# Fewer small VectorE instructions in a routing search, and one instead of two per first-layer block, in a mixture-of-experts kernel

## The chip, the cores and the metric

The kernel runs on one core of a Trainium2 chip, as one launch. The metric is the device time of the launch in microseconds (us). Before the change three runs took 705.04, 704.34 and 704.64 us; their median is 704.64 us.

## The reference

A linear attention (retention) over 8 batches, 8 heads, 576 positions and a head width of 64 gives 4,608 tokens of 512 numbers. These go through a mixture of 8 experts. Routing is global and greedy: all pairs of a token and an expert are taken in the order of falling gate value; a token goes to the expert of its first pair that finds the expert not yet full (576 tokens each). Cut to what matters:

```python
logits = x @ w_gate                       # 4608 x 8
order = np.argsort(-logits.flatten())
for idx in order:
    tok, e = (int(idx) // E, int(idx) % E)
    if assigned[tok] >= 0 or counts[e] >= cap:
        continue
    assigned[tok] = e
    counts[e] += 1
for e in range(E):
    mask = assigned == e
    h = np.maximum(x[mask] @ w1[e], 0.0)  # 512 -> 1024
    out[mask] = h @ w2[e]                 # 1024 -> 512
```

## The kernel before, in words

**Stages.** The attention runs first, to about 200 us of the profile. Its results go to a buffer in memory (xd), and the gate values stay on the chip as 36 columns of 128 tokens. Then experts are taken one after another, in the order in which they fill up. Everything from about 229 us on is the expert stage.

**An expert.** Its 576 tokens are fetched by an indirect transfer (`gather`, line 934), transposed on TensorE in five steps (`transposes`, line 945) and split there into a high and a low part: ScalarE writes the high part xh (line 958), VectorE the rest xl (line 959). The five steps take their PSUM banks in turn under the names t, h0, h1, t, h0; t exists once, so the fourth transpose waits until line 959 has emptied the bank of the first. Weights are split the same way (`conv`, line 914: two ScalarE instructions and an adding transfer issued by GpSimd). A product in full precision is then three products of parts.

The first layer (`l1`, line 963) has 16 blocks: f from 0 to 7 (128 hidden units each), s = 0 for tokens 0 to 255 and s = 1 for tokens 256 to 575. A block is 12 products on TensorE (line 984) into a bank h0 or h1, of which there are two each. ScalarE then writes the Relu's high part into hb (line 988), and VectorE the low part, the Relu less the high part (line 991): one instruction for s = 0, two for s = 1, of 256 and of 64 tokens. The low part of the last 64 tokens lies right behind their high part (columns 576 to 639), so that the second layer can take both as one operand of 128 columns.

The second layer (`l2`, line 1006) goes over five tiles of tokens, t = 0 to 4, the last with 64 tokens; each has eight groups f of three products, or two in the last tile (line 1023). ScalarE or ScalarE and VectorE (lines 1040, 1042, 1043) take the result out, and GpSimd sends it to its rows in memory.

**A round of routing.** Round p finds the expert that fills up next and its list of tokens, while TensorE works on expert p - 1. It has three parts. The search (`search`, line 285; round 0 has its own, `search_first`) finds the value at which the expert fills up, digit by digit, in seven levels of 32 or 16 candidates. In a level, VectorE makes a table G of which token reaches which candidate (`reach`, line 161); TensorE counts per expert with nine products of four columns each (line 312), which leaves four partial counts in four blocks of 32 partitions of one PSUM bank (`own`); VectorE adds them up with the (negative) room of each expert (lines 315 to 319), takes the largest over the experts (325), compares it with zero into a column copied to all four blocks of partitions (327), transposes the column (328) and adds it up to the digit j (329). The next level's values v follow (297, 307). The digits are cut out of the values once a round (lines 154, 155), most of them in level 0 behind its table, and copied to bf16 as D (304). After the last level `f` is written by four comparisons (332). Then `members` and `listing` (lines 354, 388) mark and number the tokens and write the list with counts on TensorE (381, 417), and `leave` (448) takes the expert out and looks up each token's best remaining expert (lines 455 to 206).

**What sets the order.** The program is written out in one order, and each engine works through its own part of it in that order. Where the routing's steps stand among the products of the experts is set by a planner, `Mixer` (line 845). It keeps a time for TensorE (t) and one for VectorE (v). Every three products of the first layer add 320 or 400 to t, every group of the second 650 (`adv`); every piece of VectorE work adds its cost to v (`vec`). The routing is a generator that yields, ahead of each count on TensorE, the cost of the VectorE work before it, in ns; the planner multiplies it by 1.0 for rounds 0 and 1 and by 1.2 from round 2 on, and lets the count out as soon as its t has passed the resulting due time:

```python
            d, s.pe = next(s.side)
            s.vec(d * s.slack)
            s.ready = s.v + 150
```

A level after the first is given 2050 + 19 K for K candidates (line 309). The planner also sets when the tokens are fetched, once the list is there, and when the transposes start (line 1035).

Of the kernel before, what the change touches and what calls it, by code (L numbers as in the profile page):

```python
# [10 lines left out]
F32 = mybir.dt.float32  # L11
F32R = mybir.dt.float32r
BF16 = mybir.dt.bfloat16
I32 = mybir.dt.int32
ALU = mybir.AluOpType
AF = mybir.ActivationFunctionType
AX = mybir.AxisListType
# [46 lines left out]
def widths(shifts):  # L64
    return [1 << (a - b) for a, b in zip([32] + shifts[:-1], shifts)]
# [16 lines left out]
class Route:  # L82
# [202 lines left out]
    def search(s):  # L285
        nc, V, pool, ps = s.nc, s.nc.vector, s.pool, s.ps
        SH, KK = LATER, widths(LATER)
        for _ in s.ordered():
            pass
        s.dig(0)  # L290
        for it, K in enumerate(KK):
            last = it == len(SH) - 1
            v2 = pool.tile([128, 36, 2], BF16, name="v", bufs=2)
            v = v2[:, :, 0]
            if it:

                V.tensor_scalar(v2, u[:, :, None].to_broadcast([128, 36, 2]), j, None, op0=ALU.subtract)
            else:
                V.tensor_copy(v2, s.dg[:, 0, :, None].to_broadcast([128, 36, 2]))
            s.reach(0, 36, K, v2, ALU.is_le)  # L300
            if it == 0:
                for k in range(1, 7):
                    s.dig(k)
                V.tensor_copy(s.D[:, 1:], s.dg[:, 1:])
            if not last:
                u = pool.tile([128, 36], F32, name="u")
                V.scalar_tensor_tensor(u, v, float(KK[it+1]), s.D[:, it+1], op0=ALU.mult, op1=ALU.add)

            yield (2050 + 19*K if it else 1350), 310
            cp = ps.tile([128, 32], F32, name="r")  # L310
            for c in range(0, 36, 4):
                nc.tensor.matmul(cp, s.G[:, c:c+4].rearrange("p c k -> p (c k)"), s.oh[:, c:c+4, :], start=(c == 0), stop=(c == 32))
            own = [cp[32*c:32*c+32, 8*c:8*c+8] for c in range(4)]
            cs, ct = pool.tile([32, 8], F32, name="cs"), pool.tile([32, 8], F32, name="ct4")
            V.tensor_tensor(cs, own[0], s.nr[:32], op=ALU.add)
            V.tensor_copy(ct, own[1])
            V.tensor_tensor(cs, own[2], cs, op=ALU.add)
            V.tensor_tensor(ct, own[3], ct, op=ALU.add)
            V.tensor_tensor(cs, cs, ct, op=ALU.add)
            if last:  # L320
                break

            mc, mq = pool.tile([32, 1], F32, name="mc"), pool.tile([128, 1], F32, name="mq")
            tc, j = pool.tile([128, 32], F32, name="tc"), pool.tile([128, 1], F32, name="j")
            V.tensor_reduce(mc, cs, axis=AX.X, op=ALU.max)
            for q in range(0, 128, 32):
                V.tensor_scalar(mq[q:q+32], mc, 0.0, float(KK[it+1]), op0=ALU.is_ge, op1=ALU.mult)  # L327
            V.transpose(tc, mq.to_broadcast([128, 32]))
            V.tensor_reduce(j, tc[:, 1:K], axis=AX.X, op=ALU.add)

        for q in range(0, 128, 32):
            V.tensor_scalar(s.f[q:q+32, :8], cs, 0.0, None, op0=ALU.is_ge)
        tf, cf = pool.tile([128, 32], F32, name="tc"), pool.tile([128, 32], F32, name="cf")
        nk, nf = pool.tile([128, 1], F32, name="nk"), pool.tile([128, 1], F32, name="nf")
        w = pool.tile([128, 8], F32, name="w8")
        s.ge = pool.tile([128, 2, 36], F32, name="ge")
        s.gt, s.eq = s.ge[:, 0], s.ge[:, 1]
        V.transpose(tf, s.f)
        V.tensor_reduce(nk, tf[:, :K], axis=AX.X, op=ALU.add)
        V.transpose(cf, nk.to_broadcast([128, 32]))  # L340
        V.tensor_reduce(nf, cf[:, :8], axis=AX.X, op=ALU.max)
        V.scalar_tensor_tensor(w, cf[:, :8], nf, s.dec, op0=ALU.is_equal, op1=ALU.mult)
        V.tensor_scalar(s.gt, v, nf, -1.0, op0=ALU.subtract, op1=ALU.is_gt)
        V.tensor_scalar(s.eq, v, nf, -1.0, op0=ALU.subtract, op1=ALU.is_equal)
        s.pick(w)
# [530 lines left out]
def moe(tc, nc, P, R, xd, w1_d, w2_d, out, mix):  # L876
    V, A, T = nc.vector, nc.scalar, nc.tensor
# [84 lines left out]

    def l1(e, tr):

        hb = P['w'].tile([128, 8, 1152], F32R, name="hb", bufs=1)
        order = [(f, s) for f in range(8) for s in range(2)]
        if e == 0:
            order[1:3] = order[2], order[1]
        for i, (f, s) in enumerate(order):
            wh, wl = [w.rearrange("p (f d m) -> p f d m", f=2, d=4)[:, f % 2] for w in W1[e, f // 2]]  # L970
            if i == 0 and e:
                next(tr, None)
                next(tr, None)
            elif i == 1:
                for _ in tr:
                    pass
            xh, xl = XH[e], XL[e]
            c, n = ((slice(0, 256), 256), (slice(256, 576), 320))[s]
            ps = P['ps'].tile([128, n], F32, name="ph", tag=f"h{s}", bufs=2)
            terms = [(w[:, d], x[:, d, c]) for d in range(4) for w, x in ((wh, xh), (wh, xl), (wl, xh))]  # L980
            if e == 0 and f < 2:
                terms = terms[0::3] + terms[2::3] + terms[1::3]
            for k, (w, x) in enumerate(terms):
                T.matmul(ps, w, x, start=(k == 0), stop=(k == 11))  # L984
                if k % 3 == 2:
                    mix.adv(320 + 80*s)
                    gather(e + 1)
            A.activation(hb[:, f, c], ps, AF.Relu)  # L988
            for a, b in ((0, 256),) if s == 0 else ((0, 256), (256, 320)):
                to = (640 if a == 0 else 64) + 256*s  # L990
                V.scalar_tensor_tensor(hb[:, f, to+a:to+b], ps[:, a:b], 0.0, hb[:, f, 256*s+a:256*s+b].bitcast(F32),  # L991
                                       op0=ALU.max, op1=ALU.subtract)
            mix.vec(340 + 140*s)
            if s and f in (1, 2, 4, 6) or e == 0 and i < 3:
                conv()
        return hb
# [9 lines left out]
    def l2(e, hb):  # L1006
        tr = iter(())
        late = []
        want = 4*(e + 1 < E)
        wait = 0  # L1010
        for t in range(5):
            n = 128 if t < 4 else 64
            ps = P['ps'].tile([128, DM], F32, name="py", tag="y", bufs=2)
            c = slice(128*t, 128*t+n)
            k, last = 0, 23 if t < 4 else 15
            for f in range(8):
                wh, wl = [w[:, (f % 2)*512:(f % 2)*512+512] for w in W2[e, f // 2]]

                h = hb[:, f]
                for a, w in ((h[:, c], wh), (h[:, 640+128*t:768+128*t], wh), (h[:, c], wl)) if t < 4 else \  # L1020
                        ((h[:, 512:640], wh), (h[:, c], wl)):
                    m = a.shape[1]
                    T.matmul(ps[:m], a, w, start=(k == 0), stop=(k == last), skip_group_check=True)  # L1023
                    k += 1
                mix.adv(650)
                gather(e + 1)
                wait -= 1

                soon = state['listing'] == e + 1 and not ready(e + 1)
                if want and wait <= 0 and e + 1 in regs and not soon:  # L1030
                    conv()
                    want, wait = want - 1, 6
                if late and not soon:
                    late.pop(0)()
                if e + 1 in XG and e + 1 not in XH and mix.t > state['arrives']:
                    tr = transposes(e + 1)
                next(tr, None)
            y = P['w'].tile([128, DM], F32, name="yt", bufs=3)
            if t < 4:
                A.activation(y, ps, AF.Copy)  # L1040
            else:
                A.activation(y[:n], ps[n:], AF.Copy)  # L1042
                V.tensor_tensor(y[:n], y[:n], ps[:n], op=ALU.add)  # L1043
            late.append(lambda t=t, y=y, n=n: scatter(e, t, y, n))
        for f in late:
            f()
        for _ in range(want):
            conv()
        if e + 1 < E and e + 1 not in XH:
            mix.drain(lambda: ready(e + 1))  # L1050
            gather(e + 1)
            tr = transposes(e + 1)
        return tr
# [84 lines left out]
```

## Time and profile before

| | us |
|---|---|
| median of three runs | 704.64 |
| profiled execution | 710.73 |
| its span, first to last instruction | 709.0 |
| TensorE products busy | 662.8 |
| VectorE busy | 434.9 |
| ScalarE busy | 315.4 |
| GpSimd busy | 182.7 |

The profile is one execution. Rows of its timeline give the start and the time of an instruction, its engine (PE is TensorE, DVE is VectorE, ACT is ScalarE, POOL is GpSimd), its line in the kernel, what it writes and from what, and in brackets how long the engine had stood idle before it and what ended that. Instructions of one kind in a row are merged (x4). Rows of groups give the count, the busy time and the mean of one in ns, and the idle time before them. A row of waits gives who waited for whom, the sum in us, the number of times and the longest. The granted clock is the share of TensorE's full clock that it was allowed.

### The profile page before, as it was taken

How to read it: one execution, taken by the hardware profiler on the slowest of the kernel's cores; microseconds unless marked ns; L12 is line 12 of the kernel's file. 1: busy time of each engine (PE TensorE's matmuls, PEld its weight loads, DVE VectorE, ACT ScalarE, POOL GpSimd, SP SyncE). 2: the span in 40 equal slices, each digit the busy share in tenths (PEclk: the TensorE clock that was granted, in tenths of full speed). 3: DMA queues.
4: the chain of work that ended last, by engine and by line, in shares of the span. 5: the costliest groups of instructions: out<-in, count | busy, mean ns of one | idle time of the engine just before them, and what ended most of it. 6: DMA issues, size and time to landing. Idle time of an engine off the chain costs nothing.

```text
span 709.0 us, 14398 instructions
## 1 busy us (share of the span) xinstructions
PE 662.8 (93%) x5435; PEld 578.1 (82%) x5435; DVE 434.9 (61%) x1660; ACT 315.4 (44%) x551; POOL 182.7 (26%) x236
## 2 busy tenths in 40 slices
PE   5999999999986899999999998899999999999995
PEld 5998988988764887897788778788978988988984
DVE  4456766867845698888588788769977321221200
ACT  2555555554412733555244515533551571571521
POOL 3121212122203202515213314124133233332111
PEclk9999999999966999999899999999999999999999
DMA  7986688784416754978928946884794886886421
GB/s 227 337 308 230 218 273 302 242 286 145 135 48 213 177 122 161 237 192 237 250 53 229 233 120 156 208 194 132 156 246 143 202 213 188 204 200 198 90 60 37
DMA packets 53429, 134.74 MB, mean 190 GB/s; under 512 B 6128, under 2 KB 22512, under 8 KB 53360
## 3 DMA queue, kind: packets, MB, share of 16 engines
q1 hardware_dynamic: 38400, 81.91, 34.1%
q0 software_dynamic: 14960, 51.91, 33.1%
q8 instruction: 43, 0.70, 0.4%
q14 instruction: 26, 0.21, 0.1%
HBM read 81.90 MB, written 18.87 MB: 142 GB/s over the span
## 4 chain that ended last, share of the span: by engine, by line
PE 59%; DVE 18%; issue 9%; DMA 8%; ACT 2%; SPq 2%; POOL 1%; POOLq 0%; DVEq 0%; ACTq 0%
PE py L1023 19%; PE ph L984 14%; PE pA L573 7%; PE pX L624 4%; DMA raw<-in_w 3%; PE pS L589 3%; PE pX L614 3%; DVE hb L991 2%; DMA w1l<-raw 2%; DVE G L161 2%; PE pT L653 1%; PE pT L690 1%; PE pt L956 1%; DVE mq L327 1%; PE r L270 1%
## 5 line engine op out<-in xcount | busy, mean ns | idle before, releaser
L1023 PE MATMUL py<-w2h,hb 128*128 128x512 f32 x576 | 191.1, 404 | 0.0
L984 PE MATMUL ph<-xh,w1h 128*128 128x320 f32 (+1 forms) x512 | 153.1, 303 | 4.7 <-DVE hb L991 2.5
L984 PE MATMUL ph<-xh,w1l 128*128 128x320 f32 (+1 forms) x512 | 149.5, 296 | 0.0
L984 PE MATMUL ph<-xl,w1h 128*128 128x320 f32 (+1 forms) x512 | 149.4, 296 | 0.0
L1023 PE MATMUL py<-w2l,hb 128*128 128x512 f32 (+1 forms) x320 | 126.5, 395 | 0.2 <-DMA w2l<-raw 0.2
L1023 PEld LDWEIGHTS py<-w2h,hb 128*128 128x128 f32 x576 | 105.5, 191 | 21.3
L984 PEld LDWEIGHTS ph<-xh,w1h 128*128 128x128 f32 x512 | 96.8, 190 | 6.9 <-ACT w2l L928 2.7
L988 ACT ACTIVATE hb<-ph 128x256 fp32r<-128x256 f32 (+1 forms) x128 | 51.8, 408 | 111.8 <-PE ph L984 105.2
L984 PEld LDWEIGHTS ph<-xl,w1h 128*128 128x128 f32 x512 | 96.4, 190 | 0.3
L984 PEld LDWEIGHTS ph<-xh,w1l 128*128 128x128 f32 x512 | 96.3, 189 | 0.1
L991 DVE SCALAR_TENSOR_TENSOR hb<-ph,hb 128x256 fp32r<-128x256 f32 (+1 forms) x192 | 58.5, 352 | 56.5 <-ACT hb L988 54.4
L573 PE MATMUL pA<-qin,kz 128*128 128x128 f32 x576 | 75.8, 288 | 6.7 <-DMA qin<-in_qk 5.3
L595 ACT ACTIVATE S<-pS,cst 64x128 f32<-64x128 f32 x128 | 46.4, 362 | 75.5 <-PE pS L589 73.9
L573 PEld LDWEIGHTS pA<-qin,kz 128*128 128x128 f32 x576 | 70.5, 200 | 9.2 <-ACT kz L514 7.1
L1000 POOL DMA_INDIRECT out_y<-yt,idx x40 | 40.3, 1008 | 117.2 <-ACT yt L1040 78.3
L1023 PEld LDWEIGHTS py<-w2l,hb 128*128 128x128 f32 (+1 forms) x320 | 57.6, 180 | 14.0 <-DMA w2l<-raw 0.7
L1040 ACT ACTIVATE yt<-py 128x512 f32<-128x512 f32 x32 | 19.1, 598 | 107.3 <-PE py L1023 84.4
L555 POOL TENSOR_TENSOR ks<-nin,cst 128x512 f32<-128x512 f32 (+1 forms) x33 | 33.2, 1025 | 129.5 <-DMA nin<-in_vk 85.1
L577 DVE TENSOR_TENSOR am<-pA,cst 128x512 f32<-128x512 f32 (+1 forms) x80 | 48.4, 633 | 23.9 <-PE pA L573 23.5
L929 POOL DMA_DIRECT2D w2l<-raw x32 | 28.8, 900 | 126.5 <-ACT hb L988 116.3
L940 POOL DMA_INDIRECT xg<-xd,idx x40 | 41.0, 1025 | 67.2 <-issue 30.0
L1043 DVE TENSOR_TENSOR yt<-yt,py 64x512 f32<-64x512 f32 x8 | 5.4, 678 | 69.5 <-ACT yt L1042 69.4
(179 smaller groups left out, 977.0 us busy)
## 6 DMA issues: line engine op xcount, KB each, us to landing
raw<-in_w SPq DMA_DIRECT2D x64, 512.0 KB, 5.6
w2l<-raw POOLq DMA_DIRECT2D x32, 512.0 KB
w1l<-raw POOLq DMA_DIRECT2D x31, 512.0 KB
kin<-in_qk SPq DMA_DIRECT2D x14, 576.0 KB
qin<-in_qk SPq DMA_DIRECT2D x14, 576.0 KB
vin<-in_vk SPq DMA_DIRECT2D x14, 576.0 KB, 5.3
nin<-in_vk SPq DMA_DIRECT2D x14, 512.0 KB, 5.0
xd<-xr SPq DMA_DIRECT2D x36, 192.0 KB, 3.1
```

Source lines behind the costliest of these rows:

```text
L555: nc.gpsimd.tensor_tensor(KS[u][:, a:b], LD[u, 'n'].rearrange("p (a d) -> p a d", d=64)[:, a:b], ks[:, u % HP, a:b, None].to_broadcast([12 ...
L573: nc.tensor.matmul(pa[:, j, h], KZ[u % 2][:, h, s], LD[u, 'q'][:, s], start=True, stop=True)
L577: nc.vector.tensor_tensor(am[:, :n], pa[:, :n], m[:, None, 2*hp:2*hp+2, :].to_broadcast([128, n, 2, 128]), op=ALU.mult)
L595: nc.scalar.activation(st[64*h:64*h+64, :, 64*h:64*h+64], PS[u][64*h:64*h+64], AF.Copy, scale=ss[64*h:64*h+64, hp, c:c+1])
L624: nc.tensor.matmul(px[64*h:64*h+64, :], v[:, blk*128+64*h:blk*128+64*h+64], AM[g][:, h, :], start=False, stop=blk < 8, skip_group_check=True)
L929: nc.gpsimd.dma_start(lo, raw, accum_op=ALU.add)
L940: nc.gpsimd.indirect_dma_start(out=xg[:n, j, :], out_offset=None, in_=xd[:, :], in_offset=bass.IndirectOffsetOnAxis(ap=found[e][:n, j:j+1] ...
L984: T.matmul(ps, w, x, start=(k == 0), stop=(k == 11))
L988: A.activation(hb[:, f, c], ps, AF.Relu)
L991: V.scalar_tensor_tensor(hb[:, f, to+a:to+b], ps[:, a:b], 0.0, hb[:, f, 256*s+a:256*s+b].bitcast(F32), op0=ALU.max, op1=ALU.subtract)
L1000: st = nc.gpsimd.indirect_dma_start(out=out[:, :], out_offset=bass.IndirectOffsetOnAxis(ap=found[e][:n, t:t+1], axis=0), in_=y[:n], in_off ...
L1023: T.matmul(ps[:m], a, w, start=(k == 0), stop=(k == last), skip_group_check=True)
```

## The change

In a search level three of the four partial counts are taken off the room (`cs` is then what the others leave), and the fourth is compared with that, once for each block of 32 partitions; the largest of the flags over the experts replaces the largest of the counts and the comparison with zero. The factor between levels goes from the flags to the values: D holds digits divided by K, u is a plain sum, and v is (u - j) times K. After the last level the same four comparisons stand for the ones at line 332. The planner's cost of a level falls from 2050 + 19 K to 1700 + 19 K. In the first layer, the low part of 320 tokens is one instruction; the low parts now lie together at columns 576 to 1151, and ScalarE writes the high part of the last 64 tokens a second time behind them, at columns 1152 to 1215. The second layer's operand for the last tile takes these.

```diff
@@ search
-                V.tensor_scalar(v2, u[:, :, None].to_broadcast([128, 36, 2]), j, None, op0=ALU.subtract)
+                V.tensor_scalar(v2, u[:, :, None].to_broadcast([128, 36, 2]), j, float(K), op0=ALU.subtract, op1=ALU.mult)
...
-                V.tensor_copy(s.D[:, 1:], s.dg[:, 1:])
+                for a, b in ((1, 4), (4, 7)):
+                    V.tensor_scalar(s.D[:, a:b], s.dg[:, a:b], 1.0/KK[a], None, op0=ALU.mult)
...
-                V.scalar_tensor_tensor(u, v, float(KK[it+1]), s.D[:, it+1], op0=ALU.mult, op1=ALU.add)
-
-            yield (2050 + 19*K if it else 1350), 310
+                V.tensor_tensor(u, v, s.D[:, it+1], op=ALU.add)
+
+            yield (1700 + 19*K if it else 1350), 310
...
-            cs, ct = pool.tile([32, 8], F32, name="cs"), pool.tile([32, 8], F32, name="ct4")
-            V.tensor_tensor(cs, own[0], s.nr[:32], op=ALU.add)
-            V.tensor_copy(ct, own[1])
-            V.tensor_tensor(cs, own[2], cs, op=ALU.add)
-            V.tensor_tensor(ct, own[3], ct, op=ALU.add)
-            V.tensor_tensor(cs, cs, ct, op=ALU.add)
+            cs = pool.tile([32, 8], F32, name="cs")
+            V.scalar_tensor_tensor(cs, s.nr[:32], -1.0, own[0], op0=ALU.mult, op1=ALU.subtract)
+            for x in own[1:3]:
+                V.tensor_tensor(cs, cs, x, op=ALU.subtract)
+            for q in range(0, 128, 32):
+                V.tensor_tensor(s.f[q:q+32, :8], own[3], cs, op=ALU.is_ge)
...
-            V.tensor_reduce(mc, cs, axis=AX.X, op=ALU.max)
-            for q in range(0, 128, 32):
-                V.tensor_scalar(mq[q:q+32], mc, 0.0, float(KK[it+1]), op0=ALU.is_ge, op1=ALU.mult)
+            V.tensor_reduce(mq, s.f[:, :8], axis=AX.X, op=ALU.max)
             V.transpose(tc, mq.to_broadcast([128, 32]))
             V.tensor_reduce(j, tc[:, 1:K], axis=AX.X, op=ALU.add)
...
-        for q in range(0, 128, 32):
-            V.tensor_scalar(s.f[q:q+32, :8], cs, 0.0, None, op0=ALU.is_ge)
@@ l1
-        hb = P['w'].tile([128, 8, 1152], F32R, name="hb", bufs=1)
+        hb = P['w'].tile([128, 8, 1216], F32R, name="hb", bufs=1)
...
-            for a, b in ((0, 256),) if s == 0 else ((0, 256), (256, 320)):
-                to = (640 if a == 0 else 64) + 256*s
-                V.scalar_tensor_tensor(hb[:, f, to+a:to+b], ps[:, a:b], 0.0, hb[:, f, 256*s+a:256*s+b].bitcast(F32),
-                                       op0=ALU.max, op1=ALU.subtract)
+            V.scalar_tensor_tensor(hb[:, f, 576+256*s:576+256*s+n], ps, 0.0, hb[:, f, c].bitcast(F32), op0=ALU.max, op1=ALU.subtract)
+            if s:
+                A.activation(hb[:, f, 1152:1216], ps[:, 256:320], AF.Relu)
             mix.vec(340 + 140*s)
@@ l2
-                for a, w in ((h[:, c], wh), (h[:, 640+128*t:768+128*t], wh), (h[:, c], wl)) if t < 4 else \
-                        ((h[:, 512:640], wh), (h[:, c], wl)):
+                for a, w in ((h[:, c], wh), (h[:, 576+128*t:704+128*t], wh), (h[:, c], wl)) if t < 4 else \
+                        ((h[:, 1088:1216], wh), (h[:, c], wl)):
```

More of the change, by code (lines that the diff above doesn't have):

```diff
@@ L313, in search @@
             own = [cp[32*c:32*c+32, 8*c:8*c+8] for c in range(4)]
-            cs, ct = pool.tile([32, 8], F32, name="cs"), pool.tile([32, 8], F32, name="ct4")
-            V.tensor_tensor(cs, own[0], s.nr[:32], op=ALU.add)
-            V.tensor_copy(ct, own[1])
-            V.tensor_tensor(cs, own[2], cs, op=ALU.add)
-            V.tensor_tensor(ct, own[3], ct, op=ALU.add)
-            V.tensor_tensor(cs, cs, ct, op=ALU.add)
+            cs = pool.tile([32, 8], F32, name="cs")
[4 more added lines that the diff above has]
+                V.tensor_tensor(s.f[q:q+32, :8], own[3], cs, op=ALU.is_ge)
             if last:
                 break
-            mc, mq = pool.tile([32, 1], F32, name="mc"), pool.tile([128, 1], F32, name="mq")
+            mq = pool.tile([128, 1], F32, name="mq")
             tc, j = pool.tile([128, 32], F32, name="tc"), pool.tile([128, 1], F32, name="j")
-            V.tensor_reduce(mc, cs, axis=AX.X, op=ALU.max)
-            for q in range(0, 128, 32):
-                V.tensor_scalar(mq[q:q+32], mc, 0.0, float(KK[it+1]), op0=ALU.is_ge, op1=ALU.mult)
+            V.tensor_reduce(mq, s.f[:, :8], axis=AX.X, op=ALU.max)
             V.transpose(tc, mq.to_broadcast([128, 32]))
             V.tensor_reduce(j, tc[:, 1:K], axis=AX.X, op=ALU.add)
-        for q in range(0, 128, 32):
-            V.tensor_scalar(s.f[q:q+32, :8], cs, 0.0, None, op0=ALU.is_ge)
         tf, cf = pool.tile([128, 32], F32, name="tc"), pool.tile([128, 32], F32, name="cf")
```

## The prediction

> **What bounds the kernel now.** I read the page first, then who waited for whom, with TensorE as the one that waits and from 229 us on, where the experts run:
>
> ```profile
> PE r L312 <- DVE G L161: 6.2, 9, 1.7
> PE pt L956 <- DVE xl L959: 4.5, 4, 2.0
> PE ph L984 <- DVE hb L991: 2.5, 3, 1.1
> PE ph L984 <- ACT hb L988: 1.2, 1, 1.2
> PE r L381 <- DVE sc L374: 0.9, 1, 0.9
> PE ph L984 <- ACT xh L958: 0.9, 1, 0.9
> PE r L417 <- DVE rh L413: 0.5, 1, 0.5
> ...
> ```
>
> Columns: microseconds in all, times, the longest. TensorE is hardly ever short of work in this stage: with two small ones left out, all its waits come to 17.2 us, and almost all of them are for VectorE. The change leaves every product of the expert layers as it was, so it can pay only through these waits and what they trail. Next, TensorE's and VectorE's timelines at the two longest waits for xl:
>
> ```profile
> 331.29 0.62 PE L1023 MATMUL py<-w2h,hb 128*128 128x512 f32 x2
> ...
> 331.97 0.39 PE L312 MATMUL r<-oh,G 128*128 128x32 bf16 x9
> ...
> 337.74 0.75 PE L956 MATMUL pt<-ident,xg 128*128 128x128 f32 x4 [2.00 <-DVE xl L959]
> ...
> 455.57 0.53 PE L956 MATMUL pt<-ident,xg 128*128 128x128 f32 x4 [1.88 <-DVE xl L959]
> ```
> ```profile
> 333.54 0.16 DVE L315 TENSOR_TENSOR cs<-r,room 32x8 f32<-32x8 f32 x1 [0.74 <-PE pt L956]
> ...
> 336.99 1.29 DVE L959 TENSOR_TENSOR xl<-pt,xh 128x512 fp32r<-128x512 f32 x2
> ```
>
> A level's count (331.97) goes out right ahead of the first transpose of the next expert's tokens. VectorE works through the whole level, from 333.54 to 336.99, before it comes to the first xl; the fourth transpose needs the bank which that xl empties, and waits. Then the clock falls. Windows at these two places and at a third, the granted clock third from the right, behind the busy times:
>
> ```profile
> 334.34:337.75 3.41, 1.41 (x10) 0.83 (x8) 3.13 (x13) 3.21 (x5) 2.08 (x5) 1.00 1.07 205
> 453.80:457.21 3.41, 1.64 (x11) 1.21 (x11) 3.29 (x7) 0.60 (x1) 0.00 (x0) 1.00 1.01 187
> 245.59:249.00 3.41, 1.69 (x18) 1.43 (x17) 3.02 (x16) 0.38 (x1) 0.38 (x1) 1.00 1.03 269
> 249.00:252.41 3.41, 3.41 (x34) 3.41 (x31) 3.03 (x17) 2.60 (x4) 0.00 (x0) 1.00 0.93 247
> 337.75:344.60 6.85, 6.85 (x29) 4.94 (x30) 3.03 (x9) 2.87 (x4) 1.95 (x3) 0.50 1.03 234
> 457.20:460.60 3.40, 3.40 (x10) 2.71 (x9) 0.68 (x2) 2.28 (x3) 0.70 (x2) 0.50 0.71 258
> ```
>
> After 3.41 us with only 1.41 and 1.64 of TensorE work the granted clock was 0.50, for 6.85 and 3.40 us; after a stretch with 1.69 it stayed at 1.00. Half of 6.85 and of 3.40, 5.1 us, went there. The expert stage's whole bill is thus 17.2 + 5.1 = 22.3 us.
>
> [...]
>
> **What a level costs and saves.** VectorE's rows of a level with 32 candidates, then groups by form:
>
> ```profile
> 245.14 0.42 DVE L991 SCALAR_TENSOR_TENSOR hb<-ph,hb 128x256 fp32r<-128x256 f32 x1 [2.14 <-ACT hb L988]
> 245.48 0.14 DVE L315 TENSOR_TENSOR cs<-r,room 32x8 f32<-32x8 f32 x1
> ...
> 247.26 0.21 DVE L328 STREAM_TRANSPOSE tc<-mq 128x32 f32<-128x32 f32 x1
> ```
> ```profile
> L991 DVE SCALAR_TENSOR_TENSOR hb<-ph,hb 128x256 fp32r<-128x256 f32 x128 | 52.0, 421 | 56.5 <-ACT hb L988 54.4 <-ACT w2l L928 1.6
> ...
> L991 DVE SCALAR_TENSOR_TENSOR hb<-ph,hb 128x64 fp32r<-128x64 f32 x64 | 13.7, 214 | 0.0
> ...
> L318 DVE TENSOR_TENSOR ct<-r,ct 32x8 f32<-32x8 f32 x42 | 7.0, 168 | 1.3
> ...
> L319 DVE TENSOR_TENSOR cs<-cs,ct 32x8 f32<-32x8 f32 x42 | 6.5, 154 | 1.4
> ```
>
> The ten instructions from L315 up to the transpose take 1.78 us, 0.18 each. Afterwards there are eight: three sums, four comparisons, one maximum. At 0.18 that is 1.44; the comparisons read PSUM, as L318 does (168 ns; L319, from SBUF, 154), which adds 0.06: 1.50. Saved 0.28, or 0.38 if the four, which do not wait for one another, follow at bare duration. I take 0.33, 14 us over 42 levels. The product in L307 becomes a sum and v's line gets a second scalar; no instruction is added there, so I cost both at nothing. D takes two instructions for one, 0.2 once a round by L318 and L319, behind the first count.
>
> [...]
>
> In the first layer a block of 320 tokens takes one L991 of 421 + 64/192 of (421 - 214) = 490 ns instead of 635: 0.14 saved, 9 us over 64 blocks. ScalarE gets 64 copies of 64 columns. No row shows one; the nearest are L991's forms, so between 0.21 and 0.42, and I take 0.25, near the smaller. They stand behind a Relu, where ScalarE mostly waits for TensorE. Only where a weight conversion follows (four blocks an expert) does the next Relu, and the L991 queued on it, come that much later: 0.5 us in all. Without that cover they would be 16.
>
> **Where the levels land.** VectorE's saving of some 22 us does not reach the end by itself. What counts is TensorE's order, which the planner sets, and it takes 350 ns off a level (420 from round 2 on, with its factor of 1.2), about what a level really gains. Adding up its costs with 1700 for 2050 gives the new places: round 1 ends four product groups earlier, and the lead grows to 5.8, 8.0, 9.8, 14.3 and 19.3 planner microseconds by the ends of rounds 2 to 6. Each search meets other work than before. TensorE's pace, the rows to compare with, and VectorE's tail of a listing:
>
> ```profile
> 238.92 0.31 PE L984 MATMUL ph<-xh,w1h 128*128 128x320 f32 x1
> ...
> 240.67 0.28 PE L984 MATMUL ph<-xh,w1h 128*128 128x256 f32 x1
> ...
> 242.11 0.31 PE L984 MATMUL ph<-xh,w1h 128*128 128x320 f32 x1
> ...
> 242.56 0.39 PE L312 MATMUL r<-oh,G 128*128 128x32 bf16 x9
> ...
> 248.83 0.39 PE L312 MATMUL r<-oh,G 128*128 128x32 bf16 x9 [1.72 <-DVE G L161]
> ...
> 256.98 0.39 PE L312 MATMUL r<-oh,G 128*128 128x32 bf16 x9 [0.26 <-DVE G L161]
> ...
> 260.88 0.39 PE L312 MATMUL r<-oh,G 128*128 128x32 bf16 x9 [0.22 <-DVE G L161]
> ...
> 483.51 0.85 PE L417 MATMUL r<-rh,G 128*128 128x160 bf16 x9 [0.49 <-DVE rh L413]
> ...
> 492.96 0.39 PE L312 MATMUL r<-oh,G 128*128 128x32 bf16 x9
> ...
> 498.06 0.39 PE L312 MATMUL r<-oh,G 128*128 128x32 bf16 x9 [0.54 <-DVE G L161]
> ...
> 512.82 0.47 PE L956 MATMUL pt<-ident,xg 128*128 128x128 f32 x4
> ...
> 516.57 0.54 PE L956 MATMUL pt<-ident,xg 128*128 128x128 f32 x4 [0.40 <-DVE xl L959]
> ```
> ```profile
> 489.56 0.46 DVE L206 TENSOR_TENSOR oh<-t,mx 128x288 bf16<-128x288 bf16 x1
> ...
> 490.05 1.22 DVE L991 SCALAR_TENSOR_TENSOR hb<-ph,hb 128x256 fp32r<-128x256 f32 x4
> ```
>
> First-layer blocks last 1.75 and 1.44 (238.92 to 242.11), a second-layer group 0.68 (331.29 to 331.97) or two thirds of it in the last tile; first to fourth transpose takes 3.35 unhindered (512.82 to 516.57, less 0.40).
>
> *Levels, 6.2 now.* Round 1: level 2 moves up by six products. VectorE is held until 245.14 + 0.34 by ScalarE as before, so its count comes 0.33 earlier, at 248.5; TensorE asks three quarters of a 1.75 block, one of 1.44 and a quarter of 1.75 after the last count (242.56 + 0.24), at 246.0: 2.5. The next four stand 3.0 to 3.4 apart, and VectorE needs 3.90 (256.98 to 260.88) less 0.33 and 0.14: 0.3 each. Round 1: 3.7. Level 0 to level 1 took 5.10 in the first layer (492.96 to 498.06), which becomes 4.85, and 4.3 without L991s; in round 4 the step now runs from the third product of block 11 to the sixth of block 13, in round 5 from the end of block 3 to the third of block 6, in round 6 over one whole group and four of the last tile. With the count's own 0.24 that gives TensorE 3.9, 3.8 and 2.8: 0.95, 1.05 and 1.5 of wait. Level 0 follows its listing by 9.45 (483.51 to 492.96), 8.2 without the 1.22 of L991s; round 5's now has TensorE time of 8.0 in the first layer, round 6's 7.6 in the second, round 2's 7.0 as before: 1.5, 0.6, 1.2. Other levels, by the same sums: 2.0. Together 12.5.
>
> *Transposes, 4.8 now with a small one for cs.* In experts 1 and 3 no level stands right ahead of the first transpose any more: the 2.00 and 1.88 go. But round 6's listing now stands six products before expert 4's second layer. VectorE's tail of a listing ends 6.5 us after the listing starts (483.51 to 490.02); with one L991 and one xl the bank is free at 7.6, and the fourth transpose asks at 0.7 + 0.9 + 0.7 + 3.35 = 5.6: 2.0, where 0.40 stood. Small ones elsewhere 1.1. Together 3.1.
>
> *First-layer banks, 3.7 now.* A listing or members step in the first layer holds back L991 and so a bank. Round 4's two leave the first layer; round 3 comes to the same blocks: 1.9. *Members and listings, 1.4:* both leave the spots that waited; 0.2. *Start, 1.1* as before. *ScalarE's copies* 0.5.
>
> *Clock, 5.1 now.* The waits of 2.5 and 2.0 leave 0.9 to 1.4 us of work in a window that holds them whole, more in one that splits them; two falls of 3.4 us with a chance of two thirds each: 2.3.
>
> Sum: 12.5 + 3.1 + 1.9 + 0.2 + 1.1 + 0.5 + 2.3 = 21.6 against 22.3, so 0.7 us less. This is made within the profiled execution of 710.73 us; the median of the runs is 704.64, no row tells where the 6 us between them lie, and I carry the difference over as it is: 703.9.
>
> **The rivals.** *The new level waits are half as long.* VectorE's queue ahead of a level may be shorter than in the rows I compared with. Rounds 5 and 6 then pay about half of their 5.5, and no window falls low enough for the clock: 21.6 - 2.8 - 2.3 = 16.5, 698.8 us. For it: VectorE is lighter throughout. Against: its order is fixed, and what it waits for (ScalarE at 245.14) stays.
>
> *The clock falls at the new waits as it did at 337.75.* Where expert 4's wait and round 1's leave under 1.65 us of work in their windows and the fall lasts 6.85, it costs 6.8 instead of 2.3: 26.1, 708.4, slower. For it: 2.5 and 2.0 are as long as 2.00 and 1.88. Against: 1.72 did not trip it.
>
> [...]
>
> **How the numbers follow.** A measurement of this kernel tells 0.2%, 1.4 us, from no change. My forecast, 703.9, has 0.47, on a range of its own from 701 to 706.5: 0.20 faster, 0.22 same, 0.05 slower. The halved waits have 0.27, all faster; the clock 0.18 and the comparisons 0.08, all slower. That makes 0.47 faster, 0.22 same, 0.31 slower. The range holds the first two rivals' times with about a microsecond to spare: 698 to 709.5.
>
> **What would show it.** From the first sum to the transpose 1.4 to 1.5 us instead of 1.78; L991 in a form of 320 near 490 ns; no wait near 2 us for xl in experts 1 and 3, one in expert 4; a wait near 2.5 in round 1; waits for G of about 12 us. I am wrong if those waits are not there, if the 320-wide L991 or ScalarE's copies hold banks, or if the clock falls at more than two places.

## The result and the profile after

The changed kernel takes 758.64 us (median of four runs, 756.66 to 761.76) where the kernel before took 704.49 beside it: a ratio of 1.076, 95% interval 1.072 to 1.080. It is slower by 54 us. The forecast was 703.9 with a range up to 709.5, so it failed by size and by sign. Two executions of the experiments below, one of 723.75 us with the copy first and one of 919.1 us with one column, lay more than 1.5% above the fastest of their kernel and are in no ratio.

The profiled execution took 756.66 us. Its span and mean granted clock, first after, then before, from the view of cores:

```profile
core 0: 754.9 us, clock 0.947
```
```profile
core 0: 709.0 us, clock 0.974
```

The expert stage's waits of TensorE, after the change, from 229 us on:

```profile
PE r L313 <- DVE G L161: 20.4, 16, 3.1
PE pt L954 <- DVE xl L957: 14.6, 5, 5.1
PE ph L982 <- ACT hb L989: 7.2, 3, 3.2
PE pt L954 <- DMA xg<-xd,idx: 1.5, 1, 1.5
PE ph L982 <- ACT xh L956: 0.6, 1, 0.6
PE py L1020 <- DMA w2l<-raw: 0.5, 2, 0.3
PE ph L982 <- DVE hb L987: 0.4, 2, 0.2
```

They come to 45.2 us, against 17.2 before: 28.0 more. The lower clock accounts for the rest, as an estimate from the two means: 0.053 of 754.9 is 40.0 us of lost clock, 0.026 of 709.0 is 18.4, so 21.6 more. Together that is 49.6, for a span that grew by 45.9. TensorE has the same work and is kept from it longer.

Who keeps it is shown by the second and third row of the list of all waits of the kernel after:

```profile
POOL w2l L927 <- ACT hb L986: 157.1, 31, 10.2
ACT hb L989 <- DVE hb L987: 108.2, 64, 6.5
DVE hb L987 <- ACT hb L986: 97.2, 59, 3.4
```

L989 is ScalarE's new copy of 64 columns. It waits for VectorE in each of its 64 blocks, 108.2 us in all. Before, ScalarE waited for VectorE nowhere in the first layer but once, for 2.2 us. In the trace each of the 64 copies waits for the semaphore that L987 raises; this has nothing to do with what the copy needs, which is a bank that TensorE has filled.

What one such wait does, around 387 us. ScalarE's, VectorE's and TensorE's timelines of the kernel after:

```profile
380.25 0.70 ACT L986 ACTIVATE hb<-ph 128x256 fp32r<-128x256 f32 x2
387.47 0.22 ACT L989 ACTIVATE hb<-ph 128x64 fp32r<-128x64 f32 x1 [6.53 <-DVE hb L987]
387.59 1.05 ACT L922 ACTIVATE w2h<-raw 128x1024 fp32r<-128x1024 f32 x1
388.54 1.05 ACT L926 ACTIVATE w2l<-raw 128x1024 fp32r<-128x1024 f32 x1
389.49 0.71 ACT L986 ACTIVATE hb<-ph 128x256 fp32r<-128x256 f32 x2
```
```profile
380.99 0.15 DVE L443 TENSOR_TENSOR room<-room,r 128x8 f32<-128x8 f32 x1
...
386.45 0.46 DVE L206 TENSOR_TENSOR oh<-t,mx 128x288 bf16<-128x288 bf16 x1
386.94 0.49 DVE L987 SCALAR_TENSOR_TENSOR hb<-ph,hb 128x320 fp32r<-128x320 f32 x1
389.90 0.82 DVE L987 SCALAR_TENSOR_TENSOR hb<-ph,hb 128x256 fp32r<-128x256 f32 x2 [2.46 <-ACT hb L986]
```
```profile
387.75 0.41 PE L982 MATMUL ph<-xh,w1h 128*128 128x320 f32 x1 [3.19 <-ACT hb L989]
```

It is a circle. VectorE is in the tail of a listing (380.99 to 386.91), and its L987 stands behind that. The copy waits for L987 for 6.53 us, and the two conversions and the next block's Relu stand behind the copy. VectorE, done at last, has to wait for that Relu: 2.46 us. TensorE's next block waits for the bank that the copy holds (3.19 us). Before the change ScalarE did not stop for a busy VectorE. VectorE was in the tail of a listing from 484.43 to 490.02 there, and ScalarE wrote the Relus of the next blocks as soon as TensorE had them:

```profile
487.34 0.44 ACT L988 ACTIVATE hb<-ph 128x320 fp32r<-128x320 f32 x1 [1.38 <-PE ph L984]
488.78 0.38 ACT L988 ACTIVATE hb<-ph 128x256 fp32r<-128x256 f32 x1 [1.00 <-PE ph L984]
```

The search itself did what was said of it. The first block shows a level of the kernel after on VectorE, the second two groups of its first layer:

```profile
240.96 0.14 DVE L317 SCALAR_TENSOR_TENSOR cs<-room,r 32x8 f32<-32x8 f32 x1
241.13 0.34 DVE L319 TENSOR_TENSOR cs<-cs,r 32x8 f32<-32x8 f32 x2
241.51 0.72 DVE L321 TENSOR_TENSOR f<-r,cs 32x8 f32<-32x8 f32 x4
242.26 0.16 DVE L327 TENSOR_REDUCE mq<-f 128x1 f32<-128x8 f32 x1
242.46 0.21 DVE L328 STREAM_TRANSPOSE tc<-mq 128x32 f32<-128x32 f32 x1
```
```profile
L987 DVE SCALAR_TENSOR_TENSOR hb<-ph,hb 128x320 fp32r<-128x320 f32 x64 | 31.1, 486 | 20.0 <-ACT hb L986 19.7
...
L989 ACT ACTIVATE hb<-ph 128x64 fp32r<-128x64 f32 x64 | 14.4, 224 | 108.2 <-DVE hb L987 108.2
```

From the start of the first sum to the start of the transpose it takes 1.50 us, where it was 1.78. The instruction for 320 tokens takes 486 ns and the copy 224.

### The profile page after: what moved, and what is told of

The parts are those of the page before. It is cut to its first block, busy times and chain, and to the rows that moved or that the text cites. A ratio compares the mean times of both kernels' runs of the same rounds, so it can differ in the third digit from the quotient of the medians.

```text
span 754.9 us, 14265 instructions
## 1 busy us (share of the span) xinstructions
PE 679.2 (90%) x5431; PEld 592.5 (78%) x5435; DVE 421.2 (56%) x1518; ACT 324.7 (43%) x615; POOL 182.7 (24%) x236
## 4 chain that ended last, share of the span: by engine, by line
PE 53%; DVE 23%; ACT 9%; issue 6%; DMA 5%; POOL 2%; SPq 1%; POOLq 0%; DVEq 0%; ACTq 0%
PE py L1020 20%; PE ph L982 10%; PE pA L571 6%; DVE hb L987 4%; PE pX L622 3%; PE pS L587 3%; DVE G L161 2%; DVE f L321 2%; PE pX L612 2%; ACT w2h L922 2%; ACT w2l L926 2%; DMA nin<-in_vk 2%; PE pt L954 1%; PE pT L651 1%; ACT hb L986 1%
## 5 line engine op out<-in xcount | busy, mean ns | idle before, releaser
L1020 PE MATMUL py<-w2h,hb 128*128 128x512 f32 x576 | 195.7, 413 | 0.0
L982 PE MATMUL ph<-xh,w1h 128*128 128x320 f32 (+1 forms) x512 | 157.3, 311 | 8.3 <-ACT hb L989 7.2
L982 PE MATMUL ph<-xh,w1l 128*128 128x320 f32 (+1 forms) x512 | 153.5, 304 | 0.0
L982 PE MATMUL ph<-xl,w1h 128*128 128x320 f32 (+1 forms) x512 | 153.4, 304 | 0.0
L1020 PEld LDWEIGHTS py<-w2h,hb 128*128 128x128 f32 x576 | 108.2, 196 | 22.2
L987 DVE SCALAR_TENSOR_TENSOR hb<-ph,hb 128x256 fp32r<-128x256 f32 (+1 forms) x128 | 55.4, 455 | 98.1 <-ACT hb L986 97.2
L982 PEld LDWEIGHTS ph<-xh,w1h 128*128 128x128 f32 x512 | 100.3, 197 | 10.7 <-ACT hb L989 7.9
L982 PEld LDWEIGHTS ph<-xl,w1h 128*128 128x128 f32 x512 | 100.3, 198 | 0.3
L982 PEld LDWEIGHTS ph<-xh,w1l 128*128 128x128 f32 x512 | 100.1, 197 | 0.2 <-DMA w1l<-raw 0.2
L986 ACT ACTIVATE hb<-ph 128x256 fp32r<-128x256 f32 (+1 forms) x128 | 48.6, 408 | 46.0 <-PE ph L982 43.9
L989 ACT ACTIVATE hb<-ph 128x64 fp32r<-128x64 f32 x64 | 14.4, 224 | 108.2 <-DVE hb L987 108.2
```

The costliest lines, as they stand in the source:

```text
L987: V.scalar_tensor_tensor(hb[:, f, 576+256*s:576+256*s+n], ps, 0.0, hb[:, f, c].bitcast(F32), op0=ALU.max, op1=ALU.subtract)
```

## The experiments

The theories. A: the loss is the copy's wait for VectorE. B: the search levels stand at worse places and bring the loss. C: the copy's own time on ScalarE. The twelve kernels ran in three groups of four, each group on one chip beside the kernel before (711.63, 709.42 and 704.90 us in the median), so ratios are compared. A range given in us is read as a ratio to 704.6.

**The search part alone.** The changed search and its cost of 1700, with the first layer of the kernel before:

```diff
 search(): as after the change
 l1(), l2(): as before the change
```

> The search part of the change with its planner cost of 1700, and the first layer as before. Theory A (ScalarE's new copy of 64 columns waits for VectorE in all 64 blocks, 108.2 us by the trace, and holds up ScalarE's queue): no such wait here, so the time is near the kernel before, 699 to 709 us, and waits for G are 8 to 14 us. Theory B (the search levels stand at worse places and bring the loss): 740 us or more, waits for G about 20 us as after the change. Theory C (the copies' own 14 us of ScalarE time): near 704 us too.

Measured: 718.07 us, ratio 1.009 (1.006 to 1.012). The great loss is gone, so B is not its cause. But the search part is slower than before, above the range of theory A (0.992 to 1.006). Two rows of TensorE's waits in this kernel, from 229 us on, and six rows of its timeline:

```profile
PE r L313 <- DVE G L161: 9.9, 11, 2.2
PE py L1021 <- DMA w2l<-raw: 3.6, 2, 2.4
```
```profile
248.90 0.39 PE L313 MATMUL r<-oh,G 128*128 128x32 bf16 x9 [2.25 <-DVE G L161]
...
332.45 0.80 PE L1021 MATMUL py<-w2l,hb 128*128 128x512 f32 x1 [2.44 <-DMA w2l<-raw]
...
482.40 0.39 PE L313 MATMUL r<-oh,G 128*128 128x32 bf16 x9 [0.96 <-DVE G L161]
...
495.49 0.42 PE L313 MATMUL r<-oh,G 128*128 128x32 bf16 x9 [2.04 <-issue]
...
523.47 0.53 PE L954 MATMUL pt<-ident,xg 128*128 128x128 f32 x4 [1.98 <-DVE xl L957]
...
635.25 0.66 PE L1021 MATMUL py<-w2l,hb 128*128 128x512 f32 x1 [1.21 <-DMA w2l<-raw]
```

The forecast waits of 2.5 in round 1, 1.5 at round 6's level 1 and 2.0 in expert 4's transposes are there as 2.25, 0.96 (at 482.40) and 1.98; those for xl in experts 1 and 3 are gone. The 2.04 at 495.49, in round 6's level 4, and the two waits for weights were not forecast.

**The first-layer part alone.**

```diff
 search(): as before the change, with 2050
 l1(), l2(): as after the change
```

> The first-layer part alone: one VectorE instruction for 320 tokens and ScalarE's copy, the search and its planner cost as before. Theory A: most of the 54 us, 740 to 760 us, with ScalarE's copy waiting some 100 us for VectorE. Theory B: 701 to 708 us. Theory C: 704 plus at most the copies' 14 us, 705 to 718 us.

Measured: 758.70 us, ratio 1.066 (1.063 to 1.069). ScalarE's copy waits 120.8 us for VectorE, in 62 of its 64 blocks:

```profile
ACT hb L991 <- DVE hb L989: 120.8, 62, 6.5
```

TensorE's waits for G rise from 6.2 to 22.4 us although every level stands where it stood before. A holds, B and C fall.

**The copy first.** The whole change, with two statements exchanged:

```diff
+            if s:
+                A.activation(hb[:, f, 1152:1216], ps[:, 256:320], AF.Relu)
             V.scalar_tensor_tensor(hb[:, f, 576+256*s:576+256*s+n], ps, 0.0, hb[:, f, c].bitcast(F32), ...)
-            if s:
-                A.activation(hb[:, f, 1152:1216], ps[:, 256:320], AF.Relu)
```

> The whole change, but the copy is written ahead of VectorE's instruction of the same block, so that if one of the two must wait for the other, it is VectorE that waits, for 0.22 us. Theory A: ScalarE's wait for VectorE at the copy is gone and the time falls to 701 to 711 us. Theory B: stays at 750 us or more. Theory C: the copies' 14 us are still there, so it stays above 715 us.

Measured: 714.44 us, ratio 1.004 (1.002 to 1.007), inside A's range (0.995 to 1.009) and under C's (from 1.015). The wait has turned round: the copy waits for nothing behind the Relu, and VectorE waits for the copy at 23 blocks, 24.2 us that take in the Relu ahead of it. From the view of VectorE's line:

```profile
ACT hb L988: 24.2, 23
```

The same reads of the same bank cost 7% in one order and not in the other.

**The copy from SBUF.** The whole change, the copy's source replaced:

```diff
-                A.activation(hb[:, f, 1152:1216], ps[:, 256:320], AF.Relu)
+                A.activation(hb[:, f, 1152:1216], hb[:, f, 512:576].bitcast(F32), AF.Copy)
```

> The whole change, but the copy takes the 64 columns from the high part that ScalarE has just written, not from the PSUM bank. Theory A in the form that the two wait for one another because both read one PSUM bank: the wait is gone, 700 to 709 us. Theory A in the form that they wait because both write one tile: nothing changes, 755 to 762 us. Theory B: 750 us or more in any case. Theory C: above 715 us.

Measured: 719.57 us, ratio 1.012 (1.009 to 1.015). The copy still stands behind VectorE's instruction and still writes the same columns, and it waits for nobody, in any block. So it was the read of the shared bank, not the write to the shared tile. The time lies above A's range, which ends at 1.006; the search part, which this kernel has too, loses 0.9% alone. Why it is also 0.7% slower than with the copy first, beyond both intervals, no run shows.

**One column.** The kernel before, with a read that nothing uses:

```diff
+        one = P['w'].tile([128, 1], F32, name="one", bufs=1)
...
+            if s:
+                A.activation(one, ps[:, 319:320], AF.Copy)
             mix.vec(340 + 140*s)
```

> The kernel before plus one ScalarE instruction behind VectorE's two in each block of 320 tokens, which reads one column of the block's PSUM bank into a tile that nothing uses. Theory A (it is the wait for VectorE, forced by the shared bank, not the copying): 64 waits of some 100 us in all and most of the loss, ratio 1.04 to 1.08. Theory C (the copy's work, or hb's new layout): ratio below 1.01.

Measured: 764.46 us, ratio 1.077 (1.073 to 1.080). A row of all its waits:

```profile
ACT one L995 <- DVE hb L992: 119.9, 56, 6.6
```

One column costs no less than 64 (1.066 for the first-layer part alone). It is the wait; the copy's size, the layout of hb and the one instruction for 320 tokens are not needed for the loss.

**The places of the levels.** Two kernels take apart the 0.9% of the search part. D: the cost of 1700 puts the levels at worse places. E: the new instructions hold something up.

The new search with the old cost:

```diff
-            yield (1700 + 19*K if it else 1350), 310
+            yield (2050 + 19*K if it else 1350), 310
```

> The new search with the planner's old cost of 2050, the first layer as before. Every count on TensorE stands where it stood before the change; only VectorE's work per level is shorter. Theory D (the search part alone was 0.9% slower because 1700 moves the levels to worse places): the same to 1% faster than before, ratio 0.990 to 1.000. Theory E (the new instructions themselves hold something up): ratio 1.004 or more.

Measured: 706.69 us, ratio 0.996 (0.994 to 0.998). And the kernel before with nothing but the new cost:

```diff
-            yield (2050 + 19*K if it else 1350), 310
+            yield (1700 + 19*K if it else 1350), 310
```

> The kernel before with nothing changed but the planner's cost, 1700 for 2050, so the levels stand at the new places with the old instructions. Theory D: slower than the search part alone (1.009), since each level that TensorE waits for is 0.28 us longer: 1.012 to 1.025. Theory E: 1.000 to 1.005.

Measured: 720.34 us, ratio 1.015 (1.012 to 1.018). TensorE's waits for G, first with the new search at 2050, then with the old one at 1700:

```profile
PE r L313 <- DVE G L161: 4.4, 7, 1.3
```
```profile
PE r L312 <- DVE G L161: 14.9, 18, 2.6
```

D holds: the shorter levels are worth 0.4% when the places stay, and the new places cost 1.3% with the shorter levels and 1.5% with the old ones. E falls.

**Both losses undone.** The copy first, with the planner's cost at 2050:

> The whole change with the copy ahead of VectorE's instruction and the planner's cost at 2050. Theories A and D: both losses are undone, the savings stay: ratio 0.988 to 1.000. Theory E or C: 1.004 or more.

Measured: 705.41 us, ratio 0.994 (0.991 to 0.997): 0.6% faster than the kernel before. Three more were to tell whether something better lies near it. The first has the copy first and the cost at 1900:

> As the whole change with the copy first, the planner's cost at 1900, between the change's 1700 and the old 2050. If a level's cost below what VectorE really takes is what loses (theory D as a matter of size): between the two, ratio 0.995 to 1.004. If it is the luck of where each level meets other work: anything from 0.985 to 1.010, not in order with 1700 and 2050.

Measured: 702.12 us, ratio 0.996 (0.994 to 0.998). The second has the cost at 2300:

> The same with the planner's cost at 2300. As a matter of size: fewer waits for the level's table than at 2050 (under 4 us), ratio 0.985 to 0.994. As a matter of luck: waits for xl, banks or weights take their place, 0.985 to 1.010.

Measured: 715.25 us, ratio 1.013 (1.009 to 1.017), above the ranges of both views. Waits for G fell to 3.1 us, but the first layer waited 2.84 us for xl and the second 3.19 us for a weight. Costs of 1700, 1900, 2050 and 2300 give 1.004, 0.996, 0.994 and 1.013: within the interval 1900 and 2050 are one, and both sides of them lose. For 2300 the profiled execution, 710.50 us, lies 4.7 under its median of 715.25, so its trace does not show all of the loss, and the rest stays open. The third takes the copy from SBUF, with the cost at 2050:

> The whole change with the copy taken from the high part in SBUF and the planner at 2050. VectorE does not wait for the copy here, as it does when the copy comes first: 0.22 us a block, 14 us of VectorE. If that matters, up to 0.5% faster than with the copy first (0.994); if it is covered, the same within 0.3%.

Measured: 702.34 us, ratio 0.996 (0.993 to 0.998). That is the same as with the copy first, so VectorE's wait for the copy is covered. Last, the first-layer part alone, with the copy first:

> The first-layer part alone with the copy ahead of VectorE's instruction; search and planner as before. It saves VectorE 0.14 us a block and makes it wait 0.22 for the copy. Expected: no change that can be told, 0.996 to 1.003; if the one instruction for 320 tokens were worth its 9 us of VectorE time, 0.988 to 0.993.

Measured: 704.55 us, ratio 0.9995 (0.998 to 1.001). With the wait the right way round the first-layer part is worth nothing that can be told.

## Why the prediction was wrong

**The step that failed is the price of ScalarE's copies,** 0.5 us in all. The prediction put their length between 0.21 and 0.42 us, took 0.25 (it is 0.224), and said of their place that they stand behind a Relu, "where ScalarE mostly waits for TensorE". It asked what is queued behind the copy and answered rightly (conversions, the next Relu, the L991 on it), though it gave no working for the 0.5: 32 such blocks at 0.25 would be 8. It did not ask what the copy itself waits for, and that wait was 108.2 us. It took for granted that a reader of a filled bank waits only for TensorE, and the page of before had no row to say otherwise: there the two engines read one bank too, but VectorE's read needed ScalarE's result anyway, so that a wait for the bank could not be told from a wait for the data. A wait that the change adds belongs in the sum; the first-layer part alone prices this one at 6.6% of the kernel, and the one-column run at 7.7%.

The loss had been named as a way to fail ("if the 320-wide L991 or ScalarE's copies hold banks"), but no rival carried it, so neither the range nor the chances held it. The worst of the rivals, 708.4, covers 3.8 of the 54 us.

**The search's terms were right one by one.** A level takes 1.50 us, the upper of the two values worked out (1.50 and 1.40). L991's 490 ns came as 486, and the levels of rounds 4 to 6 stand at the products that it worked out. (Its rival of halved waits takes 5.5 us for rounds 5 and 6, where the terms named for them add up to 4.65; that moves its time by 0.4 us.) PSUM as a source costs little:

```profile
L321 DVE TENSOR_TENSOR f<-r,cs 32x8 f32<-32x8 f32 x168 | 28.4, 169 | 3.1
L319 DVE TENSOR_TENSOR cs<-cs,r 32x8 f32<-32x8 f32 x84 | 13.0, 155 | 2.9
L317 DVE SCALAR_TENSOR_TENSOR cs<-room,r 32x8 f32<-32x8 f32 x42 | 6.0, 144 | 15.9 <-PE r L313 15.8
```

The seven readers of PSUM in a level (four, two and one of these rows) take 144 to 169 ns, at most 15 more than L319 of before with its 154 from SBUF. So no run shows a ground for the 0.08 that the prediction gives the comparisons: a level with them saves 0.28 us (1.78 to 1.50).

**The search's sum was wrong by about 7.5 us,** as the search part alone shows: 1.009 where the sum made it 0.998 without the copies. The sum of the waits for levels came out near the mark (for G 9.9 us and the 2.04 at 495.49, forecast 12.5), in part by luck, since the 2.04 stands in for waits that were forecast and did not come or came smaller. The waits for weights did not: 3.6 us, where the sum left them at the 0.2 of before. The larger error is the clock, 2.3 us in the sum. In every trace here the granted clock changes on one grid of 3.41 us: each low stretch that ends inside the span lasts 3.41 us or a whole multiple of it (3.41 to 13.65 in the profiles before and after). Windows of the search part alone, laid on that grid around its waits of 2.25, 2.44, 2.04, 1.98 and 1.21 us:

```profile
246.30:249.72 3.42, 1.17 (x16) 0.91 (x15) 3.16 (x14) 0.33 (x1) 0.02 (x1) 1.00 1.06 270
249.72:253.13 3.41, 3.41 (x17) 3.41 (x16) 3.08 (x15) 1.69 (x3) 0.00 (x0) 0.50 0.82 221
328.22:331.64 3.42, 1.79 (x18) 1.05 (x16) 3.12 (x19) 3.00 (x5) 1.21 (x2) 1.00 0.94 199
331.64:338.46 6.82, 6.01 (x19) 4.44 (x20) 3.59 (x10) 3.74 (x6) 1.94 (x3) 0.50 1.02 218
492.06:495.48 3.42, 1.40 (x12) 1.19 (x10) 2.46 (x13) 0.38 (x1) 1.79 (x2) 1.00 0.68 202
...
519.37:522.78 3.41, 2.12 (x14) 1.46 (x12) 3.26 (x15) 2.07 (x4) 0.86 (x1) 1.00 0.57 108
522.78:526.20 3.42, 2.73 (x16) 2.10 (x17) 3.04 (x8) 1.57 (x3) 0.00 (x0) 1.00 0.98 214
632.01:635.42 3.41, 2.20 (x12) 1.42 (x11) 1.19 (x3) 2.39 (x4) 0.13 (x1) 1.00 1.02 202
635.42:638.84 3.42, 3.42 (x9) 2.65 (x10) 0.00 (x0) 1.56 (x3) 1.44 (x3) 0.50 0.79 181
```

The clock fell after 1.17, 1.79, 1.40 and 2.20 us of work, three times for 3.41 us and once for 6.82, and half of these 17.1 us is 8.5. It did not fall after 2.12: the grid cuts the wait of 1.98 in two at 522.78. So the prediction's bound of 1.65 us is right for most windows and not sharp. In all fourteen traces, from 229 us on, the clock fell after all 48 full-clock stretches of the grid with under 1.6 us of TensorE work, after six of the 43 with 1.6 to 2.2, and after none with more. Which waits trip it could not be told beforehand, because the grid lay elsewhere in each of three profiles: here 0.71 us later after the start than in the profile before, in that of the kernel after 0.81 us earlier. Two of the four falls follow the waits for weights (331.64 and 635.42, 5.1 us); with the 3.6 us of waiting that makes 8.7, about the size of the error. The term that was mis-sized is thus the wait for weights. It comes to 2.3 to 3.6 us in the four kernels with a cost of 1700 and no wait of a copy for VectorE, and to 0.9 at most in the five such kernels with 2050. Why weights come late at the new places was not tried.

**The planner's part was foreseen only in kind.** The prediction said that the planner takes off about what a level gains, so that TensorE's order closes up and the saving does not reach the end by itself. It did not foresee that the new places lose 1.3%, nor that leaving the cost at 2050 keeps the 0.4%.

## What to carry to other kernels

Before a second engine is given a read of a bank, look up which wait it gets, and put the read ahead of the engine that is late, or take it from SBUF; 64 copies of 224 ns, 14.4 us in all on ScalarE, cost 47 us in the first-layer part alone because they stood behind a queue and had another queue behind them. When work in a hand-planned order gets shorter, change the instructions and the planner's cost in separate runs: here the instructions were worth 0.4% and the cost, moved with them, took 1.3%. A cheap operation on an idle engine still needs its list of waits written into the sum.

## What the runs showed that was not expected

The copy on ScalarE and VectorE's low part need nothing of each other, and still their reads of one PSUM bank are put in the order in which the program states them: 64 waits of 108.2 us in all in the kernel after, VectorE waiting for ScalarE when the statements are exchanged (23 waits, 24.2 us), none when the copy reads SBUF. One shared column is enough (56 waits, 119.9 us). In every one of these pairs VectorE also reads the columns that ScalarE reads, so whether reads of separate columns of a bank would wait too is not shown.

The granted clock fell to 0.50 after a wait of TensorE of only 1.21 us, while one of 1.98 that a boundary of its 3.41-us grid cut in two left it at 1.00.
